# Attention and an FFN in one kernel: the first batch's q and k with four tokens in a partition, moves of 58 rows in two parts, low parts of weights on VectorE alone

## The chip, the cores and the metric

The kernel runs on one core of a Trainium2 chip. The metric is the device time of one execution in microseconds, as the median of several runs. Engines are named as the profile names them: PE (TensorE; PEld are its weight loads), DVE (VectorE), ACT (ScalarE), POOL (GpSimd) and SP (SyncE, which here issues every DMA).

## What is computed

Eight batches, eight heads, 576 tokens, head size 64, all in float32. Attention is the sum of two parts: a pooled one, in which q, k and v are averaged over groups of four tokens and the result is repeated four times, and a local one, in which a token sees the tokens less than four places away. Behind it stand a normalisation, an FFN of 512 to 2048 to 512, and a residual.

```python
q_d = q.reshape(B, H, S // 4, 4, D).mean(axis=3)          # k_d, v_d alike
out_up = np.repeat(sm_attn(q_d, k_d, v_d), 4, axis=2)
scores = np.where(abs(i - j) < 4, q @ k.T / sqrt(D), -1e9)
x = out_up + softmax(scores) @ v                          # heads side by side: 512 wide
xn = (x - mean) / sqrt(var + 1e-6) * g_ln
out = x + relu(xn @ w_ch1) @ w_ch2
```

The FFN's weights come as 64-bit floats. The kernel reads them as pairs of 32-bit words and makes two parts of each weight, a high one and a low one; activations are split in the same way, and each FFN product is the sum of three matmuls (high by low, high by high, low by high).

## The kernel before

**Work.** The 4608 tokens are 36 tiles of 128 and 18 chunks of two tiles. For a chunk the FFN has eight pairs of hidden blocks: a pair is 24 matmuls of 256 columns (`up`, line 996, tile `h`), a ReLU with its high and low parts (lines 1003 and 1007, `hh` and `hl`), and 12 matmuls of 512 columns (`down`, line 1019, `acc`). The first two chunks run interleaved, pair by pair, while the weights are loaded and converted; all later chunks find the weights in SBUF.

**Local attention.** A batch is cut into five windows, each of two pieces of 64 tokens of which 58 are kept (`local`). Windows 0 to 6 load q and k by rows (`load_rows`, line 428: 64 tokens in 64 partitions, each head's 64 numbers a run of 256 bytes), turn them on PE (line 458) and copy them out of PSUM on ACT (line 465). Later windows load blocks of 32 tokens (line 419) and turn them on DVE (line 499). Then come the scores (lines 517 and 526, or 540), the largest, the exponentials, a turn (575), a copy (582), the product with v (596) and the division (612, 615), which leaves `xl`. v of a window is loaded by `load_v` (443, 437) into one of four buffers `vwin`.

**Pooled attention.** For the first batch the sums over four tokens are taken from the turned windows in PSUM (`sums`, line 480, four instructions for each of q and k of a window, into `gsq` and `gsk`); the pooled scores of the first batch (line 766, `gs`) need the sums of all five windows. v and the later batches are pooled on POOL (713, 714) out of loads of 72 partitions with four tokens each (line 700, `raw...`). Behind the scores follow maxima (770), exponentials (779), turns (785), copies (795) and the product with v (802, `gv`).

**Into the FFN.** The first batch's first four tiles are put together on PE (884, 890: `ex`). For later tiles the rows of `xl` are moved into the tile `x` by DMAs from SBUF to SBUF (`move`, line 662: one DMA for each half of the heads; 659 and 956 for windows turned on PE), the pooled part is loaded (865, `up`), POOL adds both (896), then come statistics, normalisation, a turn (923, `px`) and the split into `xh` and `xlo` (930, 940).

**Weights.** `weights` loads 128 rows or columns in two halves (347, 352; `s`), ACT takes the high words (359), DVE puts the low words in (367 and twice 370, `cva`), ACT makes the high part (378), and line 383 subtracts it for the low part `lo`. That last task has two possible engines, DVE and, as `alt`, POOL.

**Order.** Nothing is scheduled on the chip. Each task is added to a `Plan` with an engine, a believed duration, dependencies, a due time, the buffers that it takes and gives, and for loads a time `ahead` before which they aren't begun. `order` simulates the engines and writes out the sequence; every engine then runs its own tasks in that order and waits on semaphores. Due times come from `chunk_at` (a chunk is due every `CHUNK` = 54 us), and a task's due time is pulled forward by what depends on it. Before PE tasks that the plan sees waiting in the first 150 us it puts fill-in matmuls (line 197). 88 buffers of 2 KB a partition (`u`) serve nearly all tiles.

Of the kernel before, what the change touches and what calls it, by code (L numbers as in the profile page):

```python
# [139 lines left out]
def attention_then_ffn(  # L140
# [10 lines left out]
    nc = tc.nc  # L151
# [118 lines left out]

    T0 = 35
    C1 = 5
    CHUNK = 54
    PACE = CHUNK / NPR

    def chunk_at(c):
# [60 lines left out]
    def weights(which, f):  # L337
        key = (which, f)
        name = f"{which}_{f}"
        due = W0 + W_GAP * (f // 2) + 0.5 * (which - 1) + 1.0 * (f % 2)  # L340

        def load():
            x = box[key] = SimpleNamespace()
            x.raw = [unit([P, 512], f"s{name}_{i}", I32) for i in range(2)]
            for i in range(2):
                if which == 1:
                    nc.sync.dma_start(
                        x.raw[i].rearrange("p (c e) -> p c e", c=KC // 2),
                        w1[256 * i : 256 * (i + 1), f * 2 * P : (f + 1) * 2 * P].rearrange("(c p) e -> p c e", p=P),
                    )  # L350
# [13 lines left out]

        def low_word():
            x = box[key]
            nc.vector.tensor_single_scalar(out=x.a, in_=x.a, scalar=3, op=ALU.logical_shift_left)
            for i in range(2):
                a = x.a[:, 256 * i : 256 * (i + 1)]
                nc.vector.scalar_tensor_tensor(  # L370
                    out=a, in0=x.raw[i].rearrange("p (n two) -> p n two", two=2)[:, :, 0], scalar=29, in1=a,
                    op0=ALU.logical_shift_right, op1=ALU.bitwise_or,
                )

        def high():
            x = box[key]
            x.hi = unit([P, 512], f"hi{name}", F32R)
            nc.scalar.copy(x.hi, x.a.bitcast(F32))

        def low(eng):  # L380
            x = box[key]
            lo = unit([P, 512], f"lo{name}", F32R)
            eng.tensor_sub(lo, x.a.bitcast(F32), x.hi.bitcast(F32))
# [19 lines left out]
    last_local = SimpleNamespace(v=[None] * NVW)  # L403

    def local(i):
        b, w = divmod(i, NWIN)
# [41 lines left out]
        turned = []  # L448
        by_pe = i < NPE
        own = b < NPB  # L450
        for src, nm in ((q, "q"), (k, "k")):
            if by_pe:

                def turn(nm=nm):
# [10 lines left out]
                    nc.scalar.copy(t.rearrange("p c t -> p (c t)"), x.p[nm])  # L465
                    setattr(x, nm + "t", t)

                def sums(nm=nm):

                    for par in range(2):  # L470
                        t0 = window_start(w, par)
                        g0, g1 = (-(-(NQ * (2 * w + p)) // FACTOR) for p in (par, par + 1))
                        g1 = min(g1, SD)
                        c0 = 64 * par + FACTOR * g0 - t0
                        p = x.p[nm].rearrange("p (c t) -> p c t", c=NPAIR)
                        for hg in range(2):
                            key = (b, hg, nm)
                            if key not in gsum:
                                gsum[key] = unit([P, 2, SD], f"gs{nm}{b}_{hg}")
                            nc.vector.tensor_reduce(  # L480
                                out=gsum[key][:, :, g0:g1],
                                in_=p[:, 2 * hg : 2 * hg + 2, c0 : c0 + FACTOR * (g1 - g0)]
                                .rearrange("p c (g r) -> p c g r", r=FACTOR),
                                axis=AX.X, op=ALU.add,
                            )
# [4 lines left out]
                if own:  # L490
                    t = add("DVE", 4 * dve(120), sums, [t] + gsum_done.get((b, nm), []), due - 8.0,
                            take=() if w else (("u", 2),))
                    gsum_done.setdefault((b, nm), []).append(t)
                turned.append(add("ACT", act(512), turn_out, (t,), due - 8.0, take=U, give=A))
            else:

# [12 lines left out]
        vt = add("SP", 2.65, load_v, (last_local.v[i % NVW],), due - 8.0, lag=LAT, kb=360, ahead=AHEAD)  # L509

        def scores_by_pair():

            x.ps = [
                psa(f"ls{i}_{h2}")[:, : NPAIR * 64].rearrange("p (c j) -> p c j", c=NPAIR) for h2 in range(2)
            ]
            for h2 in range(2):
                nc.tensor.matmul(
                    x.ps[h2], lhsT=ident_b, rhs=mask_b.unsqueeze(1).broadcast_to([P, NPAIR, 64]),
                    start=True, stop=False,
                )  # L520
            for pr in range(NPAIR):
                for h2 in range(2):
                    ds = slice(64 * h2, 64 * h2 + 64)
                    for par in range(2):
                        hs = slice(64 * par, 64 * par + 64)
                        nc.tensor.matmul(
                            x.ps[h2][hs, pr], lhsT=x.qt[ds, pr, hs], rhs=x.kt[ds, pr, hs],
                            start=False, stop=pr == NPAIR - 1,
                        )

# [75 lines left out]
        def divided(h2, eng):  # L606
# [7 lines left out]
            for pr in range(NPAIR):  # L614
# [1 line left out]

        by_dve = i in SHIFTED or i >= LATE
        t = add("PE", 0.75, scores_by_pair if by_pe else scores_by_block, turned, due - 6.0,
                take=(("a", 2),), give=(("u", 2),))
# [31 lines left out]
        for e, (n, p0, r0, m, par) in enumerate(moves):  # L651

            def move(n=n, p0=p0, r0=r0, m=m, par=par):
                if n not in xt:
                    xt[n] = unit([P, DM], f"x{n}")
                to = xt[n][p0 : p0 + m]
                if by_pe:
                    r0 += 64 * par
                    nc.sync.dma_start(to, x.xl[r0 : r0 + m].rearrange("p h d -> p (h d)"))
                    return  # L660
                for h2 in range(2):
                    nc.sync.dma_start(  # L662
                        to.rearrange("p (c h d) -> p h c d", c=NPAIR, h=2)[:, h2],
                        x.xl[64 * h2 + r0 : 64 * h2 + r0 + m].rearrange("p (c n) d -> p n c d", n=2)[:, par],
                    )
# [16 lines left out]
    def pooled_half(b, hg):  # L682
# [376 lines left out]
    plan.add("POOL", 2.5, make_masks, (), 0.0)  # L1059
    choice_done = plan.add("POOL", 4.0, make_choice, (), 10.0, take=U)  # L1060
    spread_done = plan.add("POOL", 2.5, make_spread, (choice_done,), 20.0, take=U)
    for i in range(NPB * NWIN):
        local(i)
    for b in range(B):
# [51 lines left out]
```

## Time and profile before

| what | value |
|---|---|
| median of three runs | 1068.37 us (1067.54 to 1071.17) |
| the profiled execution | 1071.15 us, span 1069.4 us |
| PE busy over the span | 1040.0 us (97%) |
| DVE / ACT / POOL busy | 502.8 / 316.3 / 267.3 us |
| chain of waits: PE / DMA / SP's issuing | 76% / 9% / 5% |
| DMAs | 104.34 MB, mean 98 GB/s, 289297 packets, 237945 of them under 512 bytes |
| first matmul of the FFN | 61.2 us after the span's start |

The profile is of one execution, which was slower than the median. Busy time of PE is modelled: matmuls overlap, so a full PE is not one at its peak. The chain of waits is followed back from the last instruction, at each step to what released it. In the profile's rows a line number is a line of the kernel, and a tile's name stands without its number (`gsq` for all of q's sums). A row "x52 | 32.1, 657" is 52 instructions, busy for 32.1 us together, 657 ns one by one.

### The profile page before, as it was taken

The numbers are of one execution on the slowest core, as the hardware profiler recorded it, in microseconds if no ns is written. First come the engines' busy times: TensorE is split into PE (matmuls) and PEld (weight loads), VectorE is DVE, ScalarE is ACT, GpSimd is POOL, SyncE is SP. The second block draws the span as 40 slices with busy tenths as digits, with TensorE's granted clock in tenths as the row PEclk, the third lists the DMA queues.
The fourth block names the chain that finished last, engine by engine and source line by source line (L and its number), as shares of the span: only waits on it lengthen the run. The fifth ranks groups of instructions, "written<-read, shape, count | busy, mean of one in ns | idle before, by whom it ended". The sixth has DMA issues, their size and how long they took to land.

```text
span 1069.4 us, 23813 instructions
## 1 busy us (share of the span) xinstructions
PE 1040.0 (97%) x9290; PEld 933.8 (87%) x9290; DVE 502.8 (47%) x1304; ACT 316.3 (30%) x872; POOL 267.3 (25%) x285
## 2 busy tenths in 40 slices
PE   8988899989999999999999999999999999999998
PEld 8887788979889898989898889898898988898997
DVE  7589954434344534353444443544444444534211
ACT  5576633322322222241322132222222222212110
POOL 4234555132113221141314131132412300100000
PEclk9998999989999999999999999999999999999999
DMA  7799464534443444344453435244533333200000
GB/s 152 196 264 282 104 151 105 136 76 101 98 97 81 99 79 88 76 103 98 82 119 85 105 81 105 48 115 103 124 70 76 78 77 79 66 20 30 10 20 21
DMA packets 289297, 104.34 MB, mean 98 GB/s; under 512 B 237945, under 2 KB 276089, under 8 KB 289185
## 3 DMA queue, kind: packets, MB, share of 16 engines
q1 hardware_dynamic: 289185, 102.83, 41.3%
q8 instruction: 73, 1.20, 0.5%
q14 instruction: 39, 0.32, 0.1%
HBM read 82.58 MB, written 11.80 MB: 88 GB/s over the span
## 4 chain that ended last, share of the span: by engine, by line
PE 76%; DMA 9%; SPq 5%; DVE 4%; issue 3%; POOL 2%; ACT 2%; DVEq 0%; POOLq 0%; ACTq 0%
PE h L996 31%; PE acc L1019 30%; PE gv L802 2%; DMA x<-xl 2%; PE lv L596 2%; DMA s<-in_moe_w_ch_dram 2%; PE gs L766 2%; PE ls L540 2%; PE lt L575 2%; SPq L662 1%; PE px L923 1%; SPq L428 1%; SPq L419 1%; PE gt L785 1%; DVE cva L370 1%
## 5 line engine op out<-in xcount | busy, mean ns | idle before, releaser
L1019 PE MATMUL acc<-hi,hl 128*128 128x512 f32 x576 | 238.3, 414 | 3.2 <-DVE hl L1007 3.2
L1007 DVE SCALAR_TENSOR_TENSOR hl<-h,hh 128x512 fp32r<-128x512 f32 x144 | 98.9, 687 | 281.8 <-ACT hh L1003 253.7
L1019 PE MATMUL acc<-lo,hh 128*128 128x512 f32 x576 | 227.9, 396 | 0.0
L1019 PE MATMUL acc<-hi,hh 128*128 128x512 f32 x576 | 225.9, 392 | 0.0
L1003 ACT ACTIVATE hh<-h 128x512 fp32r<-128x512 f32 x144 | 86.3, 599 | 427.1 <-PE h L996 403.5
L996 PE MATMUL h<-xh,lo 128*128 128x256 f32 x1152 | 194.5, 291 | 0.0
L996 PE MATMUL h<-xlo,hi 128*128 128x256 f32 x1152 | 185.7, 284 | 0.0
L996 PE MATMUL h<-xh,hi 128*128 128x256 f32 x1152 | 185.6, 284 | 0.0
L996 PEld LDWEIGHTS h<-xh,lo 128*128 128x128 f32 x1152 | 169.4, 191 | 16.6
L996 PEld LDWEIGHTS h<-xlo,hi 128*128 128x128 f32 x1152 | 159.5, 193 | 0.0
L996 PEld LDWEIGHTS h<-xh,hi 128*128 128x128 f32 x1152 | 159.2, 192 | 0.0
L896 POOL TENSOR_TENSOR x<-x,up 128x512 f32<-128x512 f32 x32 | 41.2, 1288 | 377.3 <-DMA x<-xl 248.3
L1019 PEld LDWEIGHTS acc<-hi,hh 128*128 128x128 f32 x576 | 108.8, 189 | 25.2
L1019 PEld LDWEIGHTS acc<-hi,hl 128*128 128x128 f32 x576 | 109.8, 191 | 20.4 <-DVE hl L1007 4.3
L1019 PEld LDWEIGHTS acc<-lo,hh 128*128 128x128 f32 x576 | 109.9, 191 | 12.5
L930 ACT ACTIVATE xh<-px,gain 128x128 fp32r<-128x128 f32 x144 | 44.4, 372 | 75.5 <-PE px L923 35.3
L940 DVE SCALAR_TENSOR_TENSOR xlo<-px,gain,xh 128x128 fp32r<-128x128 f32 x144 | 43.0, 344 | 40.3 <-ACT xh L930 40.0
L779 ACT ACTIVATE ag<-gs,gmx 96x144 f32<-96x144 f32 x96 | 28.9, 374 | 43.2 <-DVE gmx L771 43.1
L802 PEld LDWEIGHTS gv<-vd,agt 72*72 72x72 f32 x512 | 37.2, 145 | 2.1 <-POOL mv L910 0.3
L802 PE MATMUL gv<-vd,agt 72*72 72x65 f32 x512 | 38.2, 228 | 0.2
L910 POOL TENSOR_TENSOR mv<-mv,neg_half 128x1 f32<-128x1 f32 x36 | 19.9, 554 | 73.4 <-DVE mv L907 62.9
L370 DVE SCALAR_TENSOR_TENSOR cva<-s,cva 128x256 int32<-128x256 int32 x64 | 37.5, 626 | 1.1
(191 smaller groups left out, 1129.3 us busy)
## 6 DMA issues: line engine op xcount, KB each, us to landing
s<-in_moe_w_ch_dram SPq DMA_DIRECT2D x64, 256.0 KB
vwin<-in_v_dram SPq DMA_DIRECT2D x160, 64.0 KB
out_dram<-x SPq DMA_DIRECT2D x36, 256.0 KB
qr<-in_q_dram SPq DMA_DIRECT2D x264, 32.0 KB
kr<-in_k_dram SPq DMA_DIRECT2D x264, 32.0 KB
up<-ud SPq DMA_DIRECT2D x28, 256.0 KB
x<-xl SPq DMA_DIRECT2D x66, 58.0 KB
ud<-od SPq DMA_DIRECT2D x32, 72.0 KB
```

The lines of the kernel that those rows point to most:

```text
L370: nc.vector.scalar_tensor_tensor(out=a, in0=x.raw[i].rearrange("p (n two) -> p n two", two=2)[:, :, 0], scalar=29, in1=a, op0=ALU.logical_ ...
L540: nc.tensor.matmul(x.ps[par][64 * h2 : 64 * h2 + 64, pr], lhsT=x.qt[hs, 2 * pr + h2], rhs=x.kt[hs, 2 * pr + h2], start=True, stop=True,)
L575: nc.tensor.transpose(x.pt[:, pr * P : (pr + 1) * P], x.a[:, 2 * pr : 2 * pr + 2].rearrange("p h j -> p (h j)"), ident,)
L779: nc.scalar.activation(y.a[:, c], y.ps[:, c], AF.Exp, scale=POOLED_SCALE, bias=y.mx[:, c : c + 1])
L802: nc.tensor.matmul(y.pv[:, qh, h2], lhsT=y.at[kh][:, h2, qh * GH : (qh + 1) * GH], rhs=vd[:, kh, 2 * pr + h2], start=kh == 0, stop=kh == 1,)
L896: nc.gpsimd.tensor_add(xt[n], xt[n], x.up)
L930: nc.scalar.activation(xh[c][i][:, k, j * P : (j + 1) * P], pxt[n][:, kc], AF.Copy, scale=gain[:, kc : kc + 1])
L940: nc.vector.scalar_tensor_tensor(out=xlo[c][i][:, k, ts], in0=pxt[n][:, kc], scalar=gain[:, kc : kc + 1], in1=xh[c][i][:, k, ts].bitcast(F ...
L996: nc.tensor.matmul(ph[c, p][:, fi], lhsT=wt[:, kc], rhs=xx[kc // 2][:, kc % 2], start=n == 0, stop=n == 3 * KC - 1)
L1003: nc.scalar.activation(hh[c, p], ph[c, p], AF.Relu)
L1007: nc.vector.scalar_tensor_tensor(out=hl[c, p].rearrange("p c t -> p (c t)"), in0=ph[c, p].rearrange("p c t -> p (c t)"), scalar=0.0, in1=h ...
L1019: nc.tensor.matmul(acc[c][j], lhsT=lt[:, fi, ts], rhs=rt, start=p == 0 and fi == 0 and n == 0, stop=p == NPR - 1 and fi == 1 and n == 2,)
```

## The change

Four things are changed together.

1. For the first batch, q and k are no longer loaded window by window. `own_half` loads, for each pair of heads, 80 groups of four tokens: groups 0 to 79 and groups 64 to 143, a group in a partition, so that a run is 1 KB. That is 16 loads. PE turns each with eight matmuls against the identity (one for each of the four tokens and the two heads), which write every fourth column of PSUM; DVE takes the sums over four neighbours (one instruction a load, 72 groups); ACT copies the 320 tokens out. The windows' scores then read their 64 tokens from these copies (`own_piece`), windows 0 and 1 from the first half, window 2 from both, windows 3 and 4 from the second. The pooled scores of a half of the heads wait for that half's sums alone.
2. Moves out of later windows whose number of rows has no divisor from 9 to 16 (58, 46 and 34 rows here) are cut into two parts, 58 rows into 16 and 42. A move is then four DMAs instead of two.
3. The low parts of weights have no `alt` any more: all 32 are made on DVE. Before, 13 were made on POOL.
4. The plan's numbers: `CHUNK` 56 instead of 54; the high words at 0.87 (0.668 before), the low words at 1.26 (1.109), the subtraction at 0.69 (0.599), a move at 1.8 (2.0).

```diff
-    CHUNK = 54
+    CHUNK = 56
...
-        t = add("ACT", 2 * act(256, True), high_word, (t,), due)
-        t = add("DVE", 0.45 + 2 * dve(256), low_word, (t,), due, give=(("u", 2),))
+        t = add("ACT", 0.87, high_word, (t,), due)
+        t = add("DVE", 1.26, low_word, (t,), due, give=(("u", 2),))
         t = add("ACT", act(512, True), high, (t,), due, take=U)
-        return add("DVE", dve(512), lambda: low(nc.vector), (t,), due, take=U, give=U,
-                   alt=("POOL", pool(512), lambda: low(nc.gpsimd), 0.3))
+        return add("DVE", 0.69, lambda: low(nc.vector), (t,), due, take=U, give=U)
...
+    own_t, own_done = {}, {}
+    OWN_G = ((0, 80), (SD - 80, SD))
+
+    def own_half(b, half):
+        g0, g1 = OWN_G[half]
+        ng = g1 - g0
+        add = plan.add
+        for e, (nm, src, pr) in enumerate((nm, src, pr) for pr in range(NPAIR) for nm, src in (("q", q), ("k", k))):
+            due = window_at(b * NWIN + (2 * half if half else 0)) - 8.0 + 0.2 * e
...
+            def load(x=x, nm=nm, src=src, pr=pr):
+                x.raw = unit([P, 2, FACTOR, D], f"{nm}o{b}_{pr}_{half}")[:ng]
+                nc.sync.dma_start(
+                    x.raw.rearrange("p h r d -> p h (r d)"),
+                    src[b, 2 * pr : 2 * pr + 2, FACTOR * g0 : FACTOR * g1].rearrange("h (g r) d -> g h (r d)", r=FACTOR),
+                )
+
+            def turn(x=x, nm=nm, pr=pr):
+                x.p = psa(f"l{nm}{b}_{pr}_{half}")[:, : FACTOR * ng].rearrange("p (g r) -> p g r", r=FACTOR)
+                for r in range(FACTOR):
+                    for h2 in range(2):
+                        nc.tensor.matmul(
+                            x.p[64 * h2 : 64 * h2 + 64, :, r], lhsT=x.raw[:, h2, r], rhs=ident[:ng, :ng],
+                            start=True, stop=True,
+                        )
...
+            t = add("SP", 0.5, load, (), due - 4.0, take=U, lag=LAT, kb=160, ahead=AHEAD)
+            t = add("PE", 0.5, turn, (t,), due, take=A, give=U)
+            done = gsum_done.setdefault((b, pr // 2, nm), [])
+            done.append(add("DVE", dve(288), sums, [t] + done, due + 1.0, take=() if half or pr % 2 else U))
+            own_done.setdefault((b, half), []).append(add("ACT", act(320), turn_out, (t,), due, take=U, give=A))
...
-        for src, nm in ((q, "q"), (k, "k")):
+        for src, nm in () if own else ((q, "q"), (k, "k")):
...
+                cut = max(range(0, m // 2 + 1), key=lambda a: (min(engines(a), engines(m - a)), -a)) if engines(m) < 9 else 0
                 for h2 in range(2):
-                    nc.sync.dma_start(
-                        to.rearrange("p (c h d) -> p h c d", c=NPAIR, h=2)[:, h2],
-                        x.xl[64 * h2 + r0 : 64 * h2 + r0 + m].rearrange("p (c n) d -> p n c d", n=2)[:, par],
-                    )
+                    for r1, r2 in ((0, cut), (cut, m)) if cut else ((0, m),):
+                        nc.sync.dma_start(
+                            to[r1:r2].rearrange("p (c h d) -> p h c d", c=NPAIR, h=2)[:, h2],
+                            x.xl[64 * h2 + r0 + r1 : 64 * h2 + r0 + r2].rearrange("p (c n) d -> p n c d", n=2)[:, par],
+                        )
-            t = add("SP", 0.76 if by_pe else 2.0, move, outs, due + 1.0, take=() if n in piece else U,
+            t = add("SP", 0.76 if by_pe else 1.8, move, outs, due + 1.0, take=() if n in piece else U,
...
-            ready["q"], ready["k"] = gsum_done[b, "q"], gsum_done[b, "k"]
+            ready["q"], ready["k"] = list(gsum_done[b, hg, "q"]), list(gsum_done[b, hg, "k"])
```

`engines(rows)` is the largest divisor of `rows` up to 16.

More of the change, by code (lines that the diff above doesn't have):

```diff
@@ L402, in attention_then_ffn, with sums, turn_out @@
     chosen, own_moves = {}, []
-    last_local = SimpleNamespace(v=[None] * NVW)
+    own_t, own_done = {}, {}
[6 more added lines that the diff above has]
+            due = window_at(b * NWIN + (2 * half if half else 0)) - 8.0 + 0.2 * e
+            x = SimpleNamespace()
+            def load(x=x, nm=nm, src=src, pr=pr):
[12 more added lines that the diff above has]
+                        )
+            def sums(x=x, nm=nm, pr=pr):
+                key = (b, pr // 2, nm)
+                if key not in gsum:
+                    gsum[key] = unit([P, 2, SD], f"gs{nm}{b}_{pr // 2}")
+                n0 = half * GH - g0
+                nc.vector.tensor_reduce(
+                    out=gsum[key][:, pr % 2, half * GH : (half + 1) * GH], in_=x.p[:, n0 : n0 + GH], axis=AX.X, op=ALU.add
+                )
+            def turn_out(x=x, nm=nm, pr=pr):
+                t = unit([P, 512], f"o{nm}t{b}_{pr}_{half}")
+                own_t[nm, pr, half] = t
+                nc.scalar.copy(t[:, : FACTOR * ng], x.p.rearrange("p g r -> p (g r)"))
+            t = add("SP", 0.5, load, (), due - 4.0, take=U, lag=LAT, kb=160, ahead=AHEAD)
[3 more added lines that the diff above has]
+            own_done.setdefault((b, half), []).append(add("ACT", act(320), turn_out, (t,), due, take=U, give=A))
@@ L405, in local, with own_piece, engines @@
+    def own_piece(nm, pr, w, par, ds):
+        t0 = window_start(w, par)
+        half = int(t0 + 64 > FACTOR * OWN_G[0][1])
+        t0 -= FACTOR * OWN_G[half][0]
+        return own_t[nm, pr, half][ds, t0 : t0 + 64]
+    last_local = SimpleNamespace(v=[None] * NVW, ls=None)
+    def engines(rows):
+        return max((e for e in range(1, 17) if rows and rows % e == 0), default=99)
     def local(i):
@@ L466, in turn_out @@
                     setattr(x, nm + "t", t)
[L468 to L484, printed above, removed]
-                            )
                 t = add("SP", 1.33, lambda src=src, nm=nm: load_rows(src, nm), (), due - 12.0, take=U,
@@ L489, in local @@
                 t = add("PE", 0.43, turn, (t,), due - 8.0, take=A, give=U)
[L490 to L493, printed above, removed]
                 turned.append(add("ACT", act(512), turn_out, (t,), due - 8.0, take=U, give=A))
@@ L508, in local @@
                 turned.append(add("DVE", dve(512), turn, ts, due - 8.0, take=U, give=U))
-        vt = add("SP", 2.65, load_v, (last_local.v[i % NVW],), due - 8.0, lag=LAT, kb=360, ahead=AHEAD)
+        if own:
+            for half in range(2):
+                if half in {int(window_start(w, par) + 64 > FACTOR * OWN_G[0][1]) for par in range(2)}:
+                    turned += own_done[b, half]
+            turned.append(last_local.ls)
+        vt = add("SP", 2.65 if own else 2.65, load_v, (last_local.v[i % NVW],), due - 8.0, lag=LAT, kb=360, ahead=AHEAD)
         def scores_by_pair():
@@ L520, in scores_by_pair, with of @@
                 )
+            def of(nm, pr, par, ds):
+                if own:
+                    return own_piece(nm, pr, w, par, ds)
+                return getattr(x, nm + "t")[ds, pr, 64 * par : 64 * par + 64]
             for pr in range(NPAIR):
@@ L526, in scores_by_pair @@
                         nc.tensor.matmul(
-                            x.ps[h2][hs, pr], lhsT=x.qt[ds, pr, hs], rhs=x.kt[ds, pr, hs],
+                            x.ps[h2][hs, pr], lhsT=of("q", pr, par, ds), rhs=of("k", pr, par, ds),
                             start=False, stop=pr == NPAIR - 1,
@@ L618, in local @@
         t = add("PE", 0.75, scores_by_pair if by_pe else scores_by_block, turned, due - 6.0,
-                take=(("a", 2),), give=(("u", 2),))
+                take=(("a", 2),), give=() if own and w not in (2, NWIN - 1) else (("u", 2 * NPAIR if own else 2),))
+        if own:
+            last_local.ls = t
         if not by_pe:
@@ L660, in move @@
                     return
+                cut = max(range(0, m // 2 + 1), key=lambda a: (min(engines(a), engines(m - a)), -a)) if engines(m) < 9 else 0
                 for h2 in range(2):
[L662 to L667 removed]
+                    for r1, r2 in ((0, cut), (cut, m)) if cut else ((0, m),):
+                        nc.sync.dma_start(
+                            to[r1:r2].rearrange("p (c h d) -> p h c d", c=NPAIR, h=2)[:, h2],
+                            x.xl[64 * h2 + r0 + r1 : 64 * h2 + r0 + r2].rearrange("p (c n) d -> p n c d", n=2)[:, par],
+                        )
+            t = add("SP", 0.76 if by_pe else 1.8, move, outs, due + 1.0, take=() if n in piece else U,
                     give=U if e == len(moves) - 1 else (), lag=LAT, kb=116)
@@ L1061, in attention_then_ffn @@
     spread_done = plan.add("POOL", 2.5, make_spread, (choice_done,), 20.0, take=U)
+    for b in range(NPB):
+        for half in range(2):
+            own_half(b, half)
     for i in range(NPB * NWIN):
```

## The prediction

> **What bounds the kernel now.** I read the page, then the busy time by stretch, then the chain of waits.
>
> ```profile
> span 1069.4 us, 23813 instructions
> PE 1040.0 (97%) x9290; PEld 933.8 (87%) x9290; DVE 502.8 (47%) x1304; ACT 316.3 (30%) x872; POOL 267.3 (25%) x285
> ```
>
> ```profile
> 60.00:130.00 70.00, 62.45 (x514) 55.67 (x513) 67.68 (x129) 46.50 (x127) 31.94 (x26) 0.94 0.76 216
> 130.00:190.00 60.00, 58.02 (x469) 51.39 (x470) 32.02 (x80) 22.47 (x68) 32.26 (x31) 1.00 0.54 122
> 300.00:400.00 100.00, 97.02 (x893) 87.28 (x892) 44.23 (x117) 26.31 (x74) 28.18 (x29) 0.98 0.41 91
> ```
>
> The columns are the stretch, its length, busy time (and instructions) of PE, PE's weight loads, VectorE, ScalarE and POOL, the granted clock, the DMA share and GB/s. The reader is to see three stages. By 300 us PE is all but full (97.02 of 100 us): nothing that touches another engine there can gain much. From 60 to 130 us VectorE is the bound: 67.68 of 70 us busy, while PE has 7.55 us idle and from 130 to 190 us another 1.98. Before 61 us the FFN has not begun, and the chain shows what holds it:
>
> ```profile
> 1.31 0.76 SPq L428
> 2.07 0.04 issue
> ...
> 15.35 4.11 DMA kn<-in_k_dram
> ...
> 22.57 1.48 PE gs L766 x12
> ...
> 33.04 4.30 PE gv L802 x64
> ...
> 61.40 1.43 PE h L996 x12
> ```
>
> Twenty issues at L428 (each of the five windows' q and k in two halves) follow one another on SP from 1.31 us to the last at 15.35, which lands at 19.46; three microseconds later the first pooled scores (gs) start. From there to the first FFN group at 61.4 us the order is a written one, with PE, ScalarE and VectorE taking turns. So the first 16 us belong to SP's issuing, and what follows should move with it.
>
> **The change, part by part.** All sums are against the profiled execution, 1071.15 us (span 1069.4 and 1.75 around it); that is 2.8 above the runs' median of 1068.37, and I take the same 2.8 off at the end.
>
> (1) *The first batch's q and k.* It removes 20 loads of 128 KB, 40 transposes, 40 sums and 10 copies out of PSUM, and adds 16 loads of 160 KB, 128 small matmuls, 16 sums and 16 copies.
>
> ```profile
> L700 SPq DMA_DIRECT2D raw0v<-in_v_dram x2: 370/503/636, 16.0 to 16.7; - x2
> L443 SPq DMA_DIRECT2D vwin<-in_v_dram x28: 595/607/1950, 17.2 to 66.3; - x28
> ```
>
> The twenty took 14.71 us on SP (1.31 to raw0v's first issue at 16.0), 0.74 each. No row shows the new form (80 partitions, two runs of 1 KB). The nearest is raw0v (72 partitions, four runs of 1 KB), 0.37 and 0.64; I take the middle, 0.50, as it has more runs but as many partitions, and 0.05 for the gap: 16 x 0.55 = 8.8 us, 5.9 less. Bounds: 16 x 0.42 = 6.7 (8.0 less) and 16 x 0.69 = 11.0 (3.7 less). The landing I leave at 4.1. The v loads behind them on SP (raw0v, then vwin at 0.61 each) come earlier by the same amount.
>
> The engines must keep up:
>
> ```profile
> L480 DVE TENSOR_REDUCE gsq<-lq 128x30 f32<-128x120 f32 (+2 forms) x20 | 4.1, 270 | 3.4 <-PE lq L458 3.4
> L551 DVE TENSOR_REDUCE lmx<-ls 128x4 f32<-128x256 f32 x80 | 29.7, 411 | 0.6 <-PE ls L526 0.6
> L465 ACT COPY lqt<-lq 128x512 f32<-128x512 f32 x5 | 2.9, 585 | 7.8 <-DVE gsq L480 7.7
> L795 ACT COPY agt<-gt 72x288 f32<-72x288 f32 x64 | 22.0, 407 | 26.2 <-PE gt L785 26.2
> ```
>
> Sums: 2 x 4.1 = 8.2 us go; 16 of 288 elements come, at 0.411 for 256 in L551 some 0.45 each, 7.2 us. Copies: 10 x 0.59 = 5.9 go; 16 of 320 columns come, at 0.407 for 288 some 0.43 each, 6.9 us. The matmuls: L802's 64 of 65 columns took 4.30 us, so one of 80 columns is at most 0.083 and a load's eight 0.66; with the two head halves side by side, half of that. Against a load every 0.55 us that is the pace of SP or just above it, and PE has the room: this early the planner puts fill-in matmuls before a task that waits (`warm`, up to eight). I take **-5.9 us** (bounds -8.0 and 0, the latter if something else lets gs go).
>
> (2) *Low parts of weights on VectorE alone.* Thirteen subtractions leave POOL, twelve of them between 60 and 130 us, for the engine that is the bound there.
>
> ```profile
> L370 DVE SCALAR_TENSOR_TENSOR cva<-s,cva 128x256 int32<-128x256 int32 x52 | 32.1, 657 | 0.9
> L367 DVE TENSOR_SCALAR cva<-cva 128x512 int32<-128x512 int32 x26 | 15.1, 580 | 0.0
> L383 POOL TENSOR_TENSOR lo<-cva,hi 128x512 fp32r<-128x512 f32 x12 | 16.6, 1386 | 39.1 <-ACT hi L378 23.8 <-DMA s<-in_moe_w_ch_dram 7.0 <-issue 4.4
> ...
> 93.44 0.42 DVE L367 TENSOR_SCALAR cva<-cva 128x512 int32<-128x512 int32 x1
> 93.89 2.83 DVE L370 SCALAR_TENSOR_TENSOR cva<-s,cva 128x256 int32<-128x256 int32 x2
> 98.23 0.76 DVE L370 SCALAR_TENSOR_TENSOR cva<-s,cva 128x256 int32<-128x256 int32 x2
> 98.90 0.69 DVE L383 TENSOR_TENSOR lo<-cva,hi 128x512 fp32r<-128x512 f32 x1
> ...
> 93.69 1.33 POOL L383 TENSOR_TENSOR lo<-cva,hi 128x512 fp32r<-128x512 f32 x1 [2.46 <-ACT hi L378]
> ```
>
> Added: 12 x 0.69 = 8.3 us. But a pair of L370 that takes 0.76 alone takes 2.83 beside POOL's subtraction at 93.69. Between 60 and 130 us the 26 pairs took 32.1 where 26 x 0.76 = 19.8 would do, and L367 15.1 where 26 x 0.42 = 10.9 would: 16.5 us that VectorE stood beside a busy POOL. POOL's subtractions are 16.6 of its 31.94 us, so 52% of that, 8.6 us, should go with them. Net **-0.3**; bounds +8.3 (POOL's other work stalls VectorE just as long) and -2.6 (the new ones fit in VectorE's 2.3 us of idle as well).
>
> The Trainium skill, "SBUF — State Buffer", section "Who interferes with whom", says that a VectorE instruction with two SBUF inputs and a GpSimd one that reads SBUF exclude each other for a whole instruction, whichever starts first. The rows at 93.69 and 93.89 agree. It speaks against the move too: the moved subtraction has two SBUF inputs and can itself be held by POOL's remaining work. By it each of the twelve has a chance of 15.3 in 70 (POOL's time without its subtractions) to wait some half a microsecond, +1.3: an estimate of +1 us for this part rather than -0.3.
>
> (3) *Moves of 58 rows in two parts.* By the code 58 rows become 16 + 42, and 46 and 34 rows are cut too: 66 + 6 + 6 = 78 issues more at L662.
>
> ```profile
> L662 SPq DMA_DIRECT2D x<-xl x184: 603/797/2462, 194.2 to 991.3; - x184
> L419 SPq DMA_DIRECT2D qr<-in_q_dram x264: 311/448/1644, 115.3 to 911.7; - x132
> ...
> 221.64 3.70 DMA x<-xl
> ...
> 292.30 5.21 DMA x<-xl
> ```
>
> By their records the DMA at 221.64 moves 42 rows and the one at 292.30 58. So a part should land about 1.5 us sooner. But a move's last DMA is now the fourth: it is issued 3 x 0.85 = 2.55 us after the first, where the second was at 0.85. Done after 2.55 + 3.70 = 6.25 us against 0.85 + 5.21 = 6.06: nothing gained. The price is SP's time, 78 x 0.85 = 66 us between 194 and 991 us. What hides it: SP's issues there, at their medians, are 184 x 0.80 for moves (147 us), 528 x 0.45 for q and k (264 each, 238 us), 132 vwin loads at the 0.61 above; that is 465 us, and some 190 smaller ones (raw, ud, up, out) at 0.45 make 85 more, of 797. Behind a move stand the next windows' loads, which are issued tens of microseconds ahead. I take **0**. Bounds: +1.7 on each of the few moves that reach PE, say four, +7; and the gain of the two stalls below.
>
> The Trainium skill, "DMA: Bandwidth & Descriptors", section "Why a DMA increments its semaphore by 16 and not by 1", states that a copy runs on the largest number of engines up to 16 that divides its outermost size: 2 for 58 rows, 14 for 42, 16 for 16. The two landings agree in direction. The same page's fixed cost of about 2 us a DMA would make the last part land at 2.55 + 2, 1.5 us sooner; on four moves that PE waits for, the sum would be 6 us lower.
>
> (4) *The planner's numbers* (54 to 56 us a chunk; dearer conversions). They move no work, only the order. What order can give or take:
>
> ```profile
> 232.89 1.11 PE L575 MATMUL lt<-ident,la 128*128 128x128 f32 x4 [4.88 <-ACT la L570]
> 302.74 1.20 PE L766 MATMUL gs<-ktg,qbdg 128*96 128x144 f32 x6 [2.47 <-ACT ktg L752]
> ```
>
> PE's idle time is 9.5 us between 60 and 190 and 7.35 in these two stalls. With conversions costed nearer to their rows (0.87 us for two halves on ScalarE, 1.26 for VectorE's three) attention should be put into these gaps. I take **-2**, a quarter of the two stalls; bounds -17 (all of it) and +13 (a wait of 1 us in each of 13 later chunks; the row of 300 to 400 us has 2.98 idle in less than two).
>
> Sum: -5.9 - 0.3 + 0 - 2 = -8.2: 1063.0 for a profiled execution, **1060** at the level of the median.
>
> **Rivals.**
> - *The gain at the start is hidden anyway* (chance 0.12). POOL's pooling of v, or the v windows on SP, lets gv go, not the last k. For it: gv starts 13.6 us after the landing. Against: v's loads move with SP. Start -2 instead of -5.9: 1064.
> - *VectorE eats it* (0.13). The relief of 8.6 us does not come, because POOL's other work falls on the same instructions. Then -5.9 + 8.3 = +2.4: about 1071.
> - *Slower: SP* (0.14). Where a move is followed by the next window's loads, each delayed 1.7 us, SP has no slack locally; the norm of a chunk waits for its rows and PE for the norm. It decides once SP's added work exceeds its idle stretch between two windows. One wait of 1.3 us a chunk on 13 chunks is +17: -8.2 + 17 = +8.8, 1077. Against: SP has some 245 of 797 us free, of which the 66 are a quarter.
> - *More: the stalls go as well* (0.16). The planner's truer costs take the two stalls and a few microseconds of the gaps: -8.2 - 10, 1050.
>
> **How the numbers follow.** My forecast has 0.45, the rest as above. A difference under 0.3% (3.2 us) can't be told from none. Faster: nearly all of my forecast (0.43), the larger gain (0.16) and half of the hidden one (0.06): 0.65. Same: 0.19, mostly VectorE's rival and the other half. Slower: 0.16. The forecast's own range is 1055 to 1066, from the start's bounds. The 8-in-10 range goes from 1048 (the larger gain and a little beyond) to 1071 (VectorE's rival); the SP case stays out.
>
> **What would show it.** Right: sixteen loads issued by about 10 us, gs near 17, the first FFN group near 55 to 56 instead of 61.4; L370 well below 0.657 between 60 and 130 us, with no L383 on POOL; moves of four issues that take as long as before; PE full after 300 us. Wrong: gs early but the first FFN group still near 61 (hidden); VectorE as full as before for longer (second rival); SP waits gone and PE idle before px or lt in later chunks (third).

## The result and the profile after

The changed kernel takes 1054.32 us (median of four runs, 1051.81 to 1060.49) against 1068.52 (1067.54 to 1071.17) for the kernel before on the same chip: 0.9882 of its time, 95% interval 0.9859 to 0.9904, or 12.6 us less (10.3 to 15.1; the two medians themselves differ by 14.2). Its profiled execution took 1053.27 us (span 1051.3), 1 below its median, while that of before was some 3 above. So the two traces differ by 18 us, some 4 us more than the medians.

The page of the changed kernel, its span and the busy time of the engines:

```profile
span 1051.3 us, 24104 instructions
PE 1034.3 (98%) x9450; PEld 928.9 (88%) x9450; DVE 514.0 (49%) x1301; ACT 309.8 (29%) x846; POOL 251.0 (24%) x272
```

The same three stretches as in the prediction, with the columns given there:

```profile
60.00:130.00 70.00, 64.91 (x517) 57.06 (x515) 68.49 (x130) 44.95 (x122) 28.55 (x24) 0.98 0.69 206
130.00:190.00 60.00, 58.44 (x488) 52.60 (x489) 42.16 (x90) 22.94 (x70) 22.92 (x22) 0.97 0.55 126
...
300.00:400.00 100.00, 100.00 (x909) 89.90 (x908) 45.38 (x121) 24.61 (x65) 31.43 (x32) 1.00 0.42 95
```

VectorE is still the full engine from 60 to 130 us (68.49 of 70, 67.68 before), but PE gets 2.5 us more done there, and from 300 us on it has no idle time at all, where it had 2.98 us in this stretch.

The first loads, one line for all issues of SP at the new line 419 (minimum, median and maximum of an issue in ns, first and last start):

```profile
L419 SPq DMA_DIRECT2D qo<-in_q_dram x8: 312/443/490, 1.3 to 8.7; - x8
L419 SPq DMA_DIRECT2D ko<-in_k_dram x8: 313/442/452, 1.8 to 9.3; - x8
```

And what depends on them, in the chain of waits:

```profile
17.37 1.64 PE gs L818 x12
...
30.75 4.32 PE gv L854 x64
```

The first FFN group, in PE's timeline:

```profile
54.65 0.71 PE L1048 MATMUL h<-xh,lo 128*128 128x256 f32 x4
```

Sixteen issues of 0.44 us end at 9.65 us. The pooled scores start at 17.37 (22.57 before), gv at 30.75 (33.04), the FFN at 54.65 (61.16 in the timeline of before). Not all of that is the change's: right ahead of the FFN, the profiled execution of before stood still for 3.29 us and ran its next fill-in matmuls slowly, in 2.95 us where the same ones took 1.73 in the kernel with cut moves alone:

```profile
57.55 1.11 PE L923 MATMUL px<-ident,xn 128*128 128x128 f32 x4 [3.29 <-DVE xn L914]
58.45 2.95 PE L197 MATMUL h<-ident 128*128 128x128 f32 x14
```

The profiles of the three single parts that leave the first loads as they were (below) have their first FFN group at 57.70 (cut moves), 56.85 (low parts) and 56.86 us (planner's numbers). Against these starts the change is 2.2 to 3.1 us ahead there. Counting the FFN's pairs in PE's order, the two traces are 6.5 us apart at the first, 8.9 at the 17th (at 189 us before), 13.9 at the 29th (274 us), 16.5 at the 41st (361 us) and 18.1 at the end. So 6.5 us lie before 61 us, 3.5 to 4.3 of them by the slow start of before's execution, and 7.6 between 189 and 361 us, where attention of later batches runs beside the FFN.

### The profile page after: what moved, and what is told of

Its sections match the earlier page's. It is cut to its first block, busy times and chain, and to the rows that moved or that the text cites. A ratio compares the mean times of both kernels' runs of the same rounds, so it can differ in the third digit from the quotient of the medians.

```text
span 1051.3 us, 24104 instructions
## 1 busy us (share of the span) xinstructions
PE 1034.3 (98%) x9450; PEld 928.9 (88%) x9450; DVE 514.0 (49%) x1301; ACT 309.8 (29%) x846; POOL 251.0 (24%) x272
## 4 chain that ended last, share of the span: by engine, by line
PE 83%; DVE 6%; DMA 5%; SPq 2%; issue 1%; POOL 1%; ACT 1%; ACTq 0%; DVEq 0%; POOLq 0%
PE h L1048 34%; PE acc L1071 33%; PE gv L854 3%; DMA s<-in_moe_w_ch_dram 2%; PE gs L818 2%; PE lv L643 2%; PE ls L587 2%; DVE cva L370 2%; PE lt L622 1%; PE px L975 1%; PE gt L837 1%; DVE lo L383 1%; SPq L714 1%; DMA x<-xl 1%; DVE cva L367 1%
## 5 line engine op out<-in xcount | busy, mean ns | idle before, releaser
L1079 DVE SCALAR_TENSOR_TENSOR x<-acc,x 128x512 f32<-128x512 f32 x36 | 24.7, 689 | 39.8 <-PE acc L1071 39.8
L370 DVE SCALAR_TENSOR_TENSOR cva<-s,cva 128x256 int32<-128x256 int32 x64 | 40.0, 665 | 1.1
```

Source lines behind the costliest of these rows:

```text
L370: nc.vector.scalar_tensor_tensor(out=a, in0=x.raw[i].rearrange("p (n two) -> p n two", two=2)[:, :, 0], scalar=29, in1=a, op0=ALU.logical_ ...
L1079: nc.vector.scalar_tensor_tensor(out=x, in0=acc[c][j], scalar=1.0 + 2.0**-23, in1=x, op0=ALU.mult, op1=ALU.add)
```

## The experiments

All times are medians. Each profile is of one execution, which can lie at either end of its kernel's spread. A ratio is taken against runs of the kernel before on the same chip: 1068.16 us for the first four, 1067.95 for the next four and 1068.0 for the last four. A part's worth in microseconds is its ratio times 1068. None of these kernels leaves work out.

### The four parts, each alone on the kernel before

**The first batch's loading alone.** `own_half` and `own_piece` as in the change, all else as before.

```diff
-        for src, nm in ((q, "q"), (k, "k")):
+        for src, nm in () if own else ((q, "q"), (k, "k")):
...
+    for b in range(NPB):
+        for half in range(2):
+            own_half(b, half)
```

> The kernel before with the first part of the change alone: the first batch's q and k by 16 loads of 80 groups; moves in two DMAs, low parts on POOL or VectorE, the planner's numbers all as before (CHUNK 54). By the prediction's sum: 16 issues done by about 10 us, gs near 17, the first FFN group at about 55 instead of 61.2, and that 6 us kept to the end: 1062 to 1063. Rival, the gain needs the rest: the first FFN group as early, but no more than 2 us left by the third chunk: 1066 to 1069.

Measured: 1062.48 us (1060.75 to 1065.68), ratio 0.9951 (0.9933 to 0.9970): -5.2 us, as expected. Its first FFN group came at 54.40 us.

**The low parts alone**, with the plan's order left as it was: the thirteen subtractions planned for POOL are issued to VectorE.

```diff
-                   alt=("POOL", pool(512), lambda: low(nc.gpsimd), 0.3))
+                   alt=("POOL", pool(512), lambda: low(nc.vector), 0.3))
```

> The kernel before in its own order, only that the 13 subtractions that POOL makes at L383 are issued to VectorE at the same place of the order. By the prediction's step: 8.3 us more work on VectorE between 60 and 130 us and 8.6 us less standing beside POOL, so no change: 1066 to 1070, L370's mean there falls from 657 to about 540 ns. Rival, VectorE eats it: POOL's pooling work comes earlier and stalls VectorE as long as before; L370 stays above 620 ns, and the time rises by up to 8 us: 1073 to 1077.

Measured: 1064.47 us (1062.64 to 1068.10), ratio 0.9971 (0.9957 to 0.9984): -3.1 us, faster than either range that was expected. L370 fell to 515 ns, as the step had it. Its groups on VectorE from 60 to 130 us:

```profile
L370 DVE SCALAR_TENSOR_TENSOR cva<-s,cva 128x256 int32<-128x256 int32 x54 | 25.6, 515 | 0.9
L383 DVE TENSOR_TENSOR lo<-cva,hi 128x512 fp32r<-128x512 f32 x26 | 21.2, 823 | 0.0
L367 DVE TENSOR_SCALAR cva<-cva 128x512 int32<-128x512 int32 x27 | 13.5, 500 | 0.0
```

For one piece of weight, L367 and two L370 took (15.1 + 32.1) / 26 = 1.82 us before and (13.5 + 25.6) / 27 = 1.45 here: over 26 pieces 9.6 us of relief, where the prediction had 8.6. The subtractions took 0.82 us each, not 0.69. With before's 14 subtractions on VectorE (10.0 us), the three lines cost 57.2 / 26 = 2.20 us a piece before and 60.3 / 27 = 2.23 here. So on VectorE the account is even, as forecast, and the 3.1 us must come from elsewhere. What PE waited for from 60 us to the end, the three longest sums (us in total, times, longest), in the kernel before:

```profile
PE lt L575 <- ACT la L570: 4.9, 1, 4.9
PE gs L766 <- ACT ktg L752: 3.5, 3, 2.5
PE acc L1019 <- DVE hl L1007: 3.2, 4, 1.2
```

and with the low parts on VectorE:

```profile
PE acc L1019 <- DVE hl L1007: 5.0, 4, 1.9
PE gs L766 <- ACT ktg L752: 4.3, 3, 2.5
PE lt L575 <- ACT la L570: 2.2, 1, 2.2
```

One stall shrank and two sums grew; all rows of this view together are 18.4 us before and 18.0 here. So these profiles don't show where the 3.1 us come from.

**The cut alone**, again in the order of before: the loop of the change around the moves' DMAs, and no new numbers for the plan.

```diff
+                cut = max(range(0, m // 2 + 1), key=...) if engines(m) < 9 else 0
+                    for r1, r2 in ((0, cut), (cut, m)) if cut else ((0, m),):
```

> The kernel before in its own order, only that moves of 58, 46 and 34 rows are cut in two (78 DMAs more on SP). By the prediction's step: a move lands as late as before, SP takes 66 us more of its free time: no change, 1066 to 1070. Rival from the fixed cost of a DMA: the last part lands 1.5 us sooner, the stalls at 232 and 302 us shrink: 1061 to 1064. Rival, SP is late: waits before lt, px or gs in many chunks: 1073 or more.

Measured: 1076.46 us (1072.47 to 1079.59), ratio 1.0079 (1.0056 to 1.0101): 8.4 us slower, the third of the ends expected. The profiled execution was the slowest of the six, 1079.59 us. Its chain of waits shows one place where the price falls due:

```profile
795.37 0.82 SPq L667
...
801.95 0.63 SPq L667
802.63 2.14 DMA x<-xl
...
805.87 0.56 DVE xn L919
806.43 0.14 issue
806.56 1.09 PE px L928 x4
```

and its waits of PE what comes of it (the same three sums are 3.8, 4.9 and 3.2 us in the trace of before):

```profile
PE px L928 <- DVE xn L919: 7.7, 4, 4.0
PE lt L578 <- ACT la L573: 6.5, 1, 6.5
PE acc L1024 <- DVE hl L1012: 5.3, 5, 2.1
```

The part of 42 rows lands 2.14 us after its issue, where the prediction's rows had 5.21 for 58 rows and 3.70 for 42 uncut; these are single landings. But nine issues of 0.63 to 0.87 us stand in a row on SP ahead of it, the normalisation (xn) waits for the last, and PE for that.

**The planner's numbers alone**, POOL still allowed for low parts.

```diff
-    CHUNK = 54
+    CHUNK = 56
-        t = add("ACT", 2 * act(256, True), high_word, ...)
-        t = add("DVE", 0.45 + 2 * dve(256), low_word, ...)
+        t = add("ACT", 0.87, high_word, ...)
+        t = add("DVE", 1.26, low_word, ...)
-        return add("DVE", dve(512), ...
+        return add("DVE", 0.69, ...
```

> The kernel before with the planner's numbers alone: CHUNK 56, 0.87 for the high words, 1.26 for the low words, 0.69 for the subtraction on VectorE, POOL still allowed for it. By the prediction's sum: 2 us less, from the gaps between 60 and 310 us: 1065 to 1068. Rival, the 6 us by which the change gained more than the sum are the order's: 1059 to 1063. Third, order alone is a lottery: as likely slower by 3 to 6.

Measured: 1060.98 us (1057.83 to 1065.14), ratio 0.9938 (0.9917 to 0.9958): -6.6 us. This is the rival's range. Both stalls that the prediction names are nearly gone: the waits of lt and gs near 230 and 300 us are 0.9 us each. What is longest in the rows below, the 2.2 us of gs, is another wait, at 114.5 us:

```profile
PE gs L766 <- ACT ktg L752: 3.1, 2, 2.2
...
PE lt L575 <- ACT la L570: 0.9, 1, 0.9
```

So some 5.5 of the 7.35 us went. The profiled execution was the fastest of the eight, 1057.83 us.

The four together are -5.2 - 3.1 + 8.4 - 6.6 = -6.5, against -12.6 for the changed kernel. The sum without the cut is -14.9. Taking the intervals as independent, the 6 us between -6.5 and -12.6 are uncertain by some 5.

### Parts taken out of the changed kernel

**Moves uncut.**

```diff
-                cut = max(range(0, m // 2 + 1), key=...) if engines(m) < 9 else 0
-                    for r1, r2 in ((0, cut), (cut, m)) if cut else ((0, m),):
```

> The changed kernel in its own order, only that moves are two DMAs again, uncut. If the cut costs SP the same time in this order as in the old one (8 us there), this is faster than the changed kernel: about 1046. Rival: with the rest of the change the moves sit where SP has time, or their sooner landing (2.1 us was seen for the last part, against 5.2 uncut) pays: 1053 to 1058, or slower than the changed kernel.

Measured: 1051.44 us (1047.16 to 1052.92), ratio 0.9841 (0.9819 to 0.9863): -17.0 us. That lies between the two ranges expected. So the cut costs some 4 us in the new order too; whether that is less than the 8.4 in the old one the intervals leave open. The ranges of the two kernels overlap only between 1051.8 and 1052.9.

**Every second low part on POOL**, in the order of the changed kernel.

```diff
-        return add("DVE", 0.69, lambda: low(nc.vector), ...
+        return add("DVE", 0.69, lambda: low(nc.gpsimd if f % 2 else nc.vector), ...
```

> The changed kernel in its own order, only that the low parts of weights of odd index (16 of 32) are issued to POOL at the same place. By the prediction's step VectorE loses 11 us of work and gains as much standing beside POOL: no change, 1052 to 1057. Rival, as the run that moved 13 the other way in the old order suggests (3 us faster on VectorE): 3 to 4 us slower, 1057 to 1059. Third, VectorE's relief wins: 1046 to 1050.

Measured: 1059.62 us (1055.88 to 1062.55), ratio 0.9921 (0.9897 to 0.9946), 4 to 5 us slower than the changed kernel and slower than any of the ranges expected. The sign agrees with the low parts alone, but its profile shows something that has nothing to do with them. Its turns of the first batch's q (stationary 80x64, 80 columns; each of these matmuls stands twice in the rows, so that the 64 of q are 128):

```profile
L428 PE MATMUL lq<-ident,qo 80*64 80x80 f32 x128 | 10.4, 343 | 0.0
```

The same group in the changed kernel:

```profile
L428 PE MATMUL lq<-ident,qo 80*64 80x80 f32 x128 | 6.6, 244 | 0.7 <-issue 0.7
```

In the chain a load's turn takes 1.07 us there, against 0.55, and gs starts at 24.35 instead of 17.37: PE at half speed for 20 us. Its first FFN group comes at 62.75 us, 8.1 later. So this run's 4 to 5 us can't be put down to POOL alone.

**Each own load in two DMAs**, one for each head of the pair.

```diff
-                nc.sync.dma_start(x.raw.rearrange("p h r d -> p h (r d)"), ...)
+                for h in range(2):
+                    nc.sync.dma_start(x.raw[:, h].rearrange("p r d -> p (r d)"), ...)
```

> The changed kernel in its own order, only that each of the 16 loads of the first batch's q and k is two DMAs, one a head: the same bytes in the same runs of 1 KB, but 32 issues on SP, some 7 us more. If SP's issuing sets the first scores, gs goes from 17.4 to 23 or 24 and the first FFN group is late by as much: 1059 to 1062. Rival, another wait stands behind (VectorE's sums and maxima, ScalarE waiting for the first weights): gs later, but the first FFN group by 2 us at most: 1054 to 1057.

Measured: 1061.35 us (1060.18 to 1065.51), ratio 0.9947 (0.9928 to 0.9967), 7 us slower than the changed kernel, as expected; gs starts at 23.3 us, the first FFN group at 60.94. Its issues (ns, then first and last start):

```profile
L420 SPq DMA_DIRECT2D qo<-in_q_dram x16: 422/423/1407, 1.3 to 15.9; - x16
L420 SPq DMA_DIRECT2D ko<-in_k_dram x16: 422/424/427, 2.3 to 16.9; - x16
```

An issue of half the bytes costs the same 0.42 us, so the last starts 7.6 us later. But here PE ran at half clock from 12 to 24 us (granted clock 0.50), after full speed before and a wait of 1.5 us for a load, so this run shows a price of late loads and not that of SP's issuing alone.

**CHUNK 54** in the changed kernel.

```diff
-    CHUNK = 56
+    CHUNK = 54
```

> The changed kernel with CHUNK 54 instead of 56, its other numbers kept. If the pace is what the planner's numbers gave (6 to 7 us of them together in the old kernel): 1059 to 1062, with the stalls before lt and gs near 230 and 300 us back. Rival, the dearer conversions gave it: 1052 to 1057.

Measured: 1058.44 us (1055.77 to 1059.68), ratio 0.9912 (0.9894 to 0.9931), 3 to 4 us slower than the changed kernel with overlapping ranges, and between the two ranges expected. From 200 to 330 us lt waits 0.3 us in its trace and gs 0.6 (1.2 and 0.9 in the changed kernel's), so the two stalls did not come back; a wait of px of 2.4 us stands there instead.

### PE's clock at the start, and the plan's price for a cut move

The half speed was not in any theory so far, so three of the last four kernels ask for it, and the fourth asks why the cut costs time.

**Fourteen fill-in matmuls (128x128) instead of 8 before the first own turn.**

```diff
             def turn(x=x, nm=nm, pr=pr):
+                if half == 0 and pr == 0 and nm == "q":
+                    warm[:] = [14]
```

> The changed kernel with 14 fill-in matmuls of 128x128 instead of 8 before its first own turn. Theory (clock): the own turns, matmuls of 80x64 stationary elements and 80 columns, don't bring PE from half clock to full; where the 8 fill-ins haven't done it, the turns of a load take 1.07 us instead of 0.55 and the first gs starts near 24 us instead of 17.4. Fourteen take up to 6.6 us and should always do it: turns at 0.55, gs between 17 and 18.5, median 1051 to 1054 and no run above 1057 (the changed kernel's went from 1051.8 to 1060.5). Rival (the spread is from elsewhere): median within 1 us of the changed kernel's 1054.3 and as wide a spread.

Measured: 1053.90 us (1048.79 to 1060.05), ratio 0.9871 (0.9841 to 0.9902). The turns were at full speed and gs started at 17.6 us, but the spread stayed, and the median is the changed kernel's within 0.5 us, as the rival had it. From the fastest to the slowest, the six runs had mean granted clocks of 1.000, 0.998, 0.997, 0.993, 0.994 and 0.992 at 1048.79, 1050.03, 1051.80, 1056.00, 1056.79 and 1060.05 us. So the spread goes with the granted clock. In the profiled execution (1056.0 us) the clock was at half in three places, all behind the first 20 us: from 91, from 132 and from 224 us, each beside a wait of PE of 1.6 to 3.8 us. The same wait doesn't always bring it down. Before lv near 92 us PE stood still for 2.4 us in this trace and in that of the last kernel of this section; the clock, the third number from the end, here and there:

```profile
91.50:94.50 3.00, 2.90 (x36) 2.49 (x37) 2.93 (x9) 2.11 (x7) 0.00 (x0) 0.50 0.64 160
```

```profile
91.50:94.50 3.00, 2.60 (x42) 2.28 (x43) 2.90 (x10) 2.11 (x5) 0.00 (x0) 1.00 0.69 189
```

**None**, by `warm[:] = [0]` at the same place.

> The changed kernel without the 8 fill-in matmuls before its first own turn. Theory (clock): the turns run at half speed until the 128x96 matmuls of gs, gs near 24 us, median 1058 to 1061. Rival (any matmul work of some 3.4 us brings the clock up): half speed for the first few loads only, gs by 18 to 20, median at most 1055.

Measured: 1059.84 us (1058.69 to 1061.58), ratio 0.9929 (0.9914 to 0.9944), 5 to 5.5 us slower than the changed kernel. The turns of q, and gs, without fill-ins:

```profile
L430 PE MATMUL lq<-ident,qo 80*64 80x80 f32 x128 | 10.5, 342 | 4.1 <-DMA qo<-in_q_dram 4.1
```

```profile
L820 PE MATMUL gs<-gsk,qbdg x24: 286/286/557, 23.2 to 28.3; 128*96 128x144 f32 x24
```

All 128 are slow, and gs starts at 23.2 us: as the clock theory had it, a loss as large as the whole gain of the loading alone (5.2 us).

**Uncut, with fourteen fill-ins.** Both edits from above.

> The changed kernel with uncut moves and 14 fill-ins before the first own turn. Theory (cut moves cost time on SP in the new order too, and the clock theory): 1047 to 1049, 3 to 4 below the run with 14 fill-ins and cut moves. Rival (in the new order the cut costs nothing, and the difference between cut and uncut was one of the clock at the start): equal to that run within 1 us.

Measured: 1047.73 us (1045.42 to 1050.74), ratio 0.9813 (0.9792 to 0.9834). That is 6.2 us below the cut version with fourteen fill-ins, more than the 3 to 4 expected, and the fastest median of this study.

**Cut, with fourteen fill-ins and a move planned at 3.3 us.**

```diff
-            t = add("SP", 0.76 if by_pe else 1.8, move, ...
+            t = add("SP", 0.76 if by_pe else 3.3, move, ...
```

> The changed kernel with 14 fill-ins before the first own turn and a planned SP time of 3.3 us for a move, about four issues of 0.85 with their gaps, instead of 1.8. Theory (the plan doesn't know the price of a cut move, and the stalls come from that): 1 to 3 us below the run with 14 fill-ins alone. Rival (SP's time itself costs it, and no order helps): the same as that run, or slower by the wrong guess of when PE can go on.

Measured: 1047.81 us (1045.80 to 1054.05), ratio 0.9824 (0.9800 to 0.9847), 5 to 6 us below the run with the same DMAs and a planned 1.8, where 1 to 3 were expected. Told its price, the plan seems to hide the cut; but it is no faster than uncut. Another number in the plan is also another order, and uncut moves with a planned 3.3 weren't run. So it isn't shown that the known price did it and not the new order by itself. From 190 to 300 us, the run planned with 1.8 and then the one with 3.3:

```profile
190.00:300.00 110.00, 105.54 (x930) 94.76 (x929) 43.24 (x117) 28.92 (x87) 25.25 (x26) 0.97 0.43 94
```

```profile
190.00:300.00 110.00, 110.00 (x1016) 99.00 (x1016) 47.59 (x131) 30.27 (x89) 31.45 (x32) 1.00 0.48 108
```

PE lost 4.5 us of the stretch and some of the clock (0.97) with the planned 1.8, and nothing with 3.3. (The two executions took 1056.0 and 1046.7 us, further apart than the medians.) The chain of the former shows how:

```profile
211.41 0.62 SPq L498
212.12 0.65 SPq L716
...
217.21 0.64 SPq L716
217.90 1.83 DMA x<-xl
219.85 0.69 DVE hl L1061
...
222.91 0.91 DVE lmx L602
223.90 1.75 ACT la L619 x8
```

and VectorE's timeline at the same place, with the wait ahead of the instruction in brackets:

```profile
219.85 0.69 DVE L1061 SCALAR_TENSOR_TENSOR hl<-h,hh 128x512 fp32r<-128x512 f32 x1 [11.12 <-DMA x<-xl]
```

hl is part of the FFN and reads nothing that the moves write. By the code, every tile of this size comes from one set of buffers, so what it waited for is most likely the buffer of an xl that the moves were still reading; the trace gives only the DMA that released it. Behind hl on VectorE stand the maxima (lmx), behind them ScalarE's exponentials (la), and PE stood for them:

```profile
PE lt L624 <- ACT la L619: 3.8, 1, 3.8
```

## Why the prediction was right, and where it was not

1060 was forecast and 1054.3 came, on the side forecast and inside the 8-in-10 range of 1048 to 1071, but just below the forecast's own range of 1055 to 1066. The lower end of that range doesn't follow from the start's bounds, as the text says: -8.0 in place of -5.9 gives 1058. The sum of -8.2 is close to what the four parts give alone (-6.5), but by errors that cancel, which is luck, and the whole came out faster still, at -12.6.

| step | forecast, us | measured alone, us |
|---|---|---|
| (1) loading of q and k | -5.9 (-8.0 to 0) | -5.2 |
| (2) low parts on VectorE | -0.3 (-2.6 to +8.3) | -3.1 |
| (3) moves in two parts | 0 (gain to +7) | +8.4; some +4 to +6 in the new order |
| (4) planner's numbers | -2 (-17 to +13) | -6.6 |

**(1) was right in size**, and in part by the way it named. An issue took 0.44 where 0.50 was taken, and gs came 5.2 us sooner. The turn of a load took 0.55 us, inside the estimate of 0.33 to 0.66, but only at full clock. The sentence "PE has the room" missed that at half clock it takes 1.07, and then PE and not SP sets when gs starts. The fill-ins ahead of the first turn, which the prediction named as a sign of room, are in truth what the gain rests on: without any, as much was lost. One check of "What would show it" was too good. The first FFN group was to come at 55 to 56 and came at 54.65, 6.5 us sooner; but with the cut alone, whose start is that of before, it came at 57.7:

```profile
L1001 PE MATMUL h<-xh,lo x8: 278/280/384, 57.7 to 61.0; 128*128 128x256 f32 x8
```

So about 3.5 of the 6.5 us belong to the profiled execution of before and not to the change, and the prediction took its 61.4 whole as what moves with SP's issuing. With the loading alone the group came at 54.40, 2.5 to 3.3 us ahead of the three unchanged starts. That the whole kernel gained 5.2 us (3.2 to 7.2) is measured; by which way more than these 3 us reached its end is not shown. The first rival's price, -2, lies outside that interval.

**(2) was mis-sized.** Relief and added work balance on VectorE as forecast (2.20 and 2.23 us a piece), but 3.1 us were gained, and the traces don't show where. In the changed kernel itself L370 is not relieved. Its groups from 60 to 130 us:

```profile
L370 DVE SCALAR_TENSOR_TENSOR cva<-s,cva 128x256 int32<-128x256 int32 x48 | 30.3, 673 | 0.8
L383 DVE TENSOR_TENSOR lo<-cva,hi 128x512 fp32r<-128x512 f32 x23 | 16.9, 745 | 0.2 <-ACT hi L378 0.2
```

"L370 well below 0.657" was wrong: 0.673. With the new order POOL's pooling lies beside the conversions, as the second rival had it; VectorE was as full as before, and still the kernel was faster. So the row meant to tell these cases apart didn't.

**(3) failed.** "What hides it" was a count of SP's free time over 800 us (66 of 245 us). The count holds, and decides nothing: at a move, seven to nine issues stand in a row, and xn, or through a buffer hl, waits for the last. That is the third rival's mechanism, "SP has no slack locally"; in the two places shown, the issues in a row are those of the moves themselves and not the next window's loads. Its price alone, 8.4 us, is half of its 17, and the other parts outweighed it, so that its end on the slower side didn't come. The rule of the Trainium skill that was weighed there ("DMA: Bandwidth & Descriptors", section "Anatomy of one DMA — SWDGE (gpsimd) path": a fixed cost of about 2 us a DMA, fitted there for DMAs issued from GpSimd, where these are issued by SP) is near the landings of 2.14 and 1.83 us; the gain of 6 us that was worked out from it did not come.

**(4) was mis-sized**: a quarter of the two stalls was taken, and 6.6 us came. In the trace both stalls are nearly gone (5.5 of 7.35 us), which is the fourth rival's mechanism. The step also priced a stall at its idle time alone. Behind the 4.88 us before lt, the trace of before has half clock (0.50, third number from the end) as well, which the plan's numbers alone don't have there:

```profile
232.00:238.00 6.00, 5.11 (x17) 4.41 (x18) 0.69 (x1) 3.09 (x13) 0.72 (x1) 0.50 0.10 15
```

Why the parts together give 6 us more than their sum is open. The cut may cost less in the new order (4 to 6 us for 8.4), and with a planned 3.3 us for a move the kernel was as fast as uncut. How much of (4) is CHUNK and how much the conversions' numbers stays open too; with CHUNK 54 the loss was 3 to 4 us, near what the overlap of the runs allows to say.

## What to carry to other kernels

Free time of a queue, summed over a kernel, hides nothing by itself: look at how many issues stand in a row ahead of the DMA that somebody waits for, and at who needs the buffer that it reads. Where an order is planned, a change of what a task costs belongs in the plan together with the change; here the run that had it was 5 to 6 us faster, as much as the whole loading gave, though another new order might have done the same. Before a trace of before is taken as the starting point, compare its stages with a second profile of the same program: here some 4 us of the start were one execution's. A gain at the start of a kernel should be checked against PE's clock, by the duration of equal matmuls and not by the granted clock alone.

## What the runs showed of the hardware

**A wait of PE can cost more than its length.** Behind some of its waits the granted clock reads 0.50 for some microseconds (from 232 to 238 us behind the 4.88 us before lt in the kernel before), and whether it falls differs between executions: behind the same 2.4 us before lv it was 0.50 in one trace and 1.00 in another.

**Small matmuls didn't bring PE to full clock.** In the run with half the low parts on POOL, the turns keep PE busy without a break from 6 to 16 us. That line's matmuls alone (busy time and instructions of PE and of its weight loads, granted clock, DMA share, GB/s):

```profile
6.00:16.00 10.00, 10.00 (x156) 10.00 (x154) 1.00 1.04 238
```

and in the changed kernel:

```profile
6.00:16.00 10.00, 8.32 (x218) 7.82 (x212) 1.00 1.05 235
```

156 instructions in 10 us against 218 in 8.32, with a granted clock of 1.00 in both rows, so that column doesn't show half speed where PE hasn't reached full speed yet. The Trainium skill, "TensorE: Matmul & The Clock Gate", section "Part 1: The HAM clock gate", says that PE goes to full clock after a busy window of about 3.4 us. The trace disagrees for these matmuls, which use 80 rows and 64 columns of the array: some 20 us of them left the clock at half, and full speed came only behind the first gs (128 rows, 96 columns). That the size is what matters wasn't tried by itself. Up to there these two kernels have the same program, so 8 fill-ins are enough sometimes: of the six profiles with the new loading and 8 fill-ins, five reached full speed within the first two loads and one (low parts on POOL) didn't. Two of the five lost it again between the turns, behind waits of 0.9 to 1.5 us for a load: uncut moves for 3 of the 16 loads, two issues for 9. There the column does show it; in the latter, PE was busy without a break and stayed at 0.50:

```profile
12.00:16.00 4.00, 4.00 (x64) 4.00 (x63) 1.37 (x3) 1.44 (x4) 0.00 (x0) 0.50 0.64 168
```

With 14, all three profiles ran the turns at full speed.

**An issue costs the same for half the bytes**: 0.42 us for a DMA of 80 runs of 1 KB, 0.44 for one of 160.
